# Written order of the tail columns and the first output products, one transfer for the last block

## The chip, the cores and the metric

The kernel runs on one core of one Trainium2 chip. The metric is the device time of one execution in microseconds (us). Before the change three timed runs gave 408.18, 406.88 and 407.25 us, a median of 407.25 us. Beside them one more execution was profiled; every row below is of that one.

## The reference

Three layers follow each other on 4 batches of 576 tokens, all in 32-bit floats: an attention through 32 memory slots per head, an expert layer in which each token has one of 8 experts, and a gated feed-forward layer. The change is in the third layer, and in the second a load of the first is cut in two. Cut to what matters:

```python
# attention, per batch and head (q, k, v: 576 x 64, phi: 576 x 32)
a = softmax(phi over the tokens);  k_m, v_m = a.T @ k, a.T @ v
x = softmax(q @ k_m.T / 8) @ v_m                  # 8 heads side by side: 576 x 512
# experts: e is the token's own best, or that of the token before it
x[s] = p[e] * (relu(x[s] @ w1[e]) @ w2[e])        # 512 -> 1024 -> 512
# gated layer
h = relu(x @ w_in)                                # 512 -> 1024 columns
conv = sum over k of conv_w[k] * h[s + k - 1]     # 3 taps along the tokens, zero at both ends
out = (h * sigmoid(conv)) @ w_out                 # 1024 -> 512
```

## The kernel before

**How the work is tiled.** Every product with 32-bit accuracy is three matmuls: an operand is split into a high part (rounded, by ScalarE) and a low part (the rest, by VectorE, in a few places by GpSimd), and high times high, high times low and low times high are added up (`split`, L153, and `matmul3`, L157). For most tiles the low part is thus ready some time after the high one. The expert layer leaves its result in DRAM (`ydram`), 512 rows by 576 tokens per batch.

**The gated stage** (`gated`, L1048) handles a batch in two steps. `columns` (L1072) makes the 1024 columns of `h` in eight groups of 128, f = 0 to 7: twelve matmuls into one bank `pi0_f` of PSUM for batch 0, an eviction with relu (L1085), three taps (L1066, L1068, L1069), a sigmoid (L1098), a product (`gate`, L1099), and a split of the result into the tile `g0_f` (L154 the high part, L155 the low). Then `product` (L1141) multiplies the eight tiles `g` with `w_out`: per chunk c of 128 tokens eight groups of three matmuls into a bank `po0_c`. The bank is evicted (L1173) and stored (L1175).

**The tail.** A batch has 576 tokens, and a main block takes 512 of them. The last 64 of all four batches (with two neighbours each, 264 columns) are done together, after the main columns of batch 0: eight groups of twelve matmuls into banks `pit_0` to `pit_7`, with their own evictions `htt` (L1085), taps and splits into `tail` and `edge`. The banks of `pi0` and `pit` share four buffers, so `pit_5` must wait until `pit_1` has been evicted. The token at the edge of a main block is copied into `g` from `edge` by GpSimd (`close_main`, L1121); only the last chunk of 128 tokens, c = 3, reads it.

**What sets the order.** Each engine works through its own queue in order, and a waiting instruction holds up all behind it. Up to the gated stage the matmuls' order is written out in a table. In the gated stage a scheduler places the instructions by its own estimate of when their operands are ready, unless `tc.keep_in_program_order` holds them to the order of the code (`pin`). Before the change the main columns of batch 0 and the whole products of batch 3 are held so; the tail's columns and the first products of batch 0 are not, and the scheduler mixes them. Products of c = 0 to 2 with f = 0 to 5 may run before the tail is done.

**Loads of the attention.** `load_kv` (L348) brings keys and values, 1 MB for each of 8 units; units 0 to 3 come in two transfers, the others in one.

**The end.** The last block (batch 3, c = 3) goes into a bank of its own, `last`. Behind a branch for a case that doesn't arise here (`more`, L1188) ScalarE evicts it in two halves of 256 columns (L1198), and SyncE stores each half (L1199).

Of the kernel before, what the change touches and what calls it, by code (L numbers as in the profile page):

```python
# [117 lines left out]
def fused_kernel(tc, q, first, first_q, kv, kv_tail, phi, w1, w2, w_in, conv_w, w_out, out):  # L118
# [3 lines left out]
    with (  # L122
# [225 lines left out]
        def load_kv(u):  # L348

            t = kvs[u] = ap.tile([128, 4, 4, 128], F32, tag="kv", bufs=KB, name=f"kv{u}")  # L350
            with behind(needed_behind(u // 2)):
                if u < 4:
                    for i in range(2):
                        nc.sync.dma_start(t[:, 2 * i:2 * i + 2].rearrange("p c h n -> p (c h n)"), kv[u, i])
                else:
                    nc.sync.dma_start(t.rearrange("p (i c) h n -> p i (c h n)", i=2), kv[u].rearrange("i p n -> p i n"))
                if u % 2 == 0:

                    ends[u // 2] = ap.tile([128, 4, 128], F32, tag="kt", bufs=2, name=f"kt{u // 2}")
                    nc.sync.dma_start(ends[u // 2].rearrange("p h n -> p (h n)"), kv_tail[u // 2])  # L360
# [549 lines left out]
        def load_y(b, e):  # L910

            y = state.tile([128, 4, S], F32, tag="ay", name=f"y{b}")
            nc.sync.dma_start(y[:, :, :MT], ydram[b].rearrange("d p s -> p d s")[:, :, :MT])
            return y[:, :, :MT], load_p(b, e, b, MT)[:, :MT] if e is not None else None
# [14 lines left out]
        def split_tails(yp, nm):  # L929
            y, p = yp  # L930
            t = state.tile([128, 2, 4, B * TW], F32R, tag="ay", name=f"ts{nm}")
            parts = [t[:, i] for i in range(2)]
            if p is not None:
                nc.vector.tensor_tensor(y, y, p.rearrange("p (o s) -> p o s", o=1).to_broadcast([128, 4, B * TW]), ALU.mult)
            split(*parts, y)
            return parts
# [111 lines left out]
        def gated(gp, nm, scaled=False):  # L1048
            def first(b):
                return None if scaled else expert(b)  # L1050
# [56 lines left out]
            for b in range(B):  # L1107
# [13 lines left out]
                def close_main(f):  # L1121
                    nc.gpsimd.tensor_copy(gs[f][:, :, MT - 1:], edge[:, f, :, b:b + 1].bitcast(F32))
# [2 lines left out]
                    while len(wo) < 4 and f >= WO[len(wo)]:  # L1125
                        wo.append(w2_piece(f"wo{len(wo)}", slow(f"wo.{len(wo)}")))

                columns(f"{nm}{b}", ys, store_main, tc.keep_in_program_order if b == 0 else lambda ins: ins, between)
                if b == 0:
                    tails = split_tails(tails, nm)  # L1130
                    yn = load_y(1, first(1))
                    columns(f"{nm}t", tails, store_tail)
                    for f in range(8):
                        close_main(f)
                if b + 1 < B:
                    ys = y_parts(b + 1)
                    split_y(b + 1, yn, *ys)

                pin = tc.keep_in_program_order if b == B - 1 else lambda ins: ins

                def product(ps, c, fr):  # L1141
                    for f in fr:
# [5 lines left out]
                                                                    start=f == 0 and i == 0, stop=f == 7 and i == 2)).ins]  # L1148

                chunks = [0, 1, 2] + [4] * (b % 2) + [3]  # L1150
                pss = {c: bank(f"po{b}_{c}") for c in chunks[:3]}
                for c in chunks[:3]:
                    product(pss[c], c, range(0, 6))
                for c in chunks:
                    if c in pss:
                        product(pss[c], c, range(6, 8))
# [31 lines left out]
        with tc.If(any_more > 0, preferred_fallthrough_block=True, label="more"):  # L1188
# [3 lines left out]
                    other_experts(b)  # L1192
            with tc.tile_pool(name="again", bufs=8, reuse_waits="tile") as gp:
                gated(gp, "x", True)
        for cq in range(2):
            cols = slice(256 * cq, 256 * cq + 256)
            ot = late[1].tile([128, 256], F32, tag="last", bufs=2, name=f"ot_{cq}")
            nc.scalar.activation(ot, last_block[0][:, cols], AF.Copy)  # L1198
            nc.sync.dma_start(out[B - 1, 384:512, cols], ot)  # L1199
        last_cm[0].__exit__(None, None, None)  # L1200
        late[0].__exit__(None, None, None)

# [50 lines left out]
```

## Time and profile before

| what | us |
|---|---|
| profiled execution, whole | 406.64 |
| its span, first to last instruction | 404.8 |
| median of the three timed runs | 407.25 |
| TensorE busy (matmuls) | 397.6 |
| VectorE busy | 282.9 |
| ScalarE busy | 228.1 |
| GpSimd busy | 65.4 |

The profiled execution is 1.84 us longer than its span. It is 0.61 us below the median of the timed runs. TensorE is PE in the rows, its weight loads PEld, VectorE DVE, ScalarE ACT, GpSimd POOL, and SyncE's queue, which issues most transfers, SPq. A row of a timeline gives the start in us from the start of the span, the duration in us, the engine, the line, the operation with the tile it writes and those it reads, and in brackets how long the engine was idle before it and what ended that. PE works through the columns and products of batch 0 and the tail from 204 to 259 us.

### The profile page before, as it was taken

How to read it: one execution, taken by the hardware profiler on the slowest of the kernel's cores; microseconds unless marked ns; L12 is line 12 of the kernel's file. 1: busy time of each engine (PE TensorE's matmuls, PEld its weight loads, DVE VectorE, ACT ScalarE, POOL GpSimd, SP SyncE). 2: the span in 40 equal slices, each digit the busy share in tenths (PEclk: the TensorE clock that was granted, in tenths of full speed). 3: DMA queues.
4: the chain of work that ended last, by engine and by line, in shares of the span. 5: the costliest groups of instructions: out<-in, count | busy, mean ns of one | idle time of the engine just before them, and what ended most of it. 6: DMA issues, size and time to landing. Idle time of an engine off the chain costs nothing. (4 is left out here: it accounts for less than half of the span.)

```text
span 404.8 us, 7759 instructions
## 1 busy us (share of the span) xinstructions
PE 397.6 (98%) x2969; PEld 344.2 (85%) x2970; DVE 282.9 (70%) x545; ACT 228.1 (56%) x457; POOL 65.4 (16%) x128
## 2 busy tenths in 40 slices
PE   7999999999999999999999999999999999999996
PEld 3469989899989998999988988888888888888884
DVE  3689898897868996786868999479600895069500
ACT  4466567565576366465757748468422882268311
POOL 1000201412023211311100313304100041002200
PEclk9999999999999999999999999999999999999999
DMA  7999988999196959945313033200011000200022
GB/s 265 350 397 406 361 276 307 407 414 413 46 324 211 373 147 400 389 162 171 105 61 115 26 105 104 104 2 1 2 78 52 2 0 0 104 2 0 3 80 57
DMA packets 26525, 69.03 MB, mean 171 GB/s; under 512 B 5904, under 2 KB 6672, under 8 KB 26480
## 3 DMA queue, kind: packets, MB, share of 16 engines
q1 hardware_dynamic: 22896, 56.92, 39.4%
q0 software_dynamic: 3584, 11.54, 7.2%
q8 instruction: 25, 0.41, 0.4%
q14 instruction: 20, 0.16, 0.1%
HBM read 52.12 MB, written 16.33 MB: 169 GB/s over the span
## 5 line engine op out<-in xcount | busy, mean ns | idle before, releaser
L167 PE MATMUL py<-h,wb 128*128 128x288 f32 x768 | 104.7, 296 | 0.0
L167 PEld LDWEIGHTS py<-h,wb 128*128 128x128 f32 x768 | 102.4, 188 | 0.7 <-issue 0.5
L1147 PE MATMUL po<-wo,g 128*128 128x512 f32 x360 | 83.0, 390 | 0.0
L167 PE MATMUL pi<-yh,wi 128*128 128x512 f32 x256 | 79.5, 389 | 0.0
L1147 PEld LDWEIGHTS po<-wo,g 128*128 128x128 f32 x360 | 67.4, 188 | 14.0
L167 PEld LDWEIGHTS pi<-yh,wi 128*128 128x128 f32 x256 | 48.1, 188 | 10.0
L1068 DVE SCALAR_TENSOR_TENSOR ct<-ht,convw,ct 128x510 f32<-128x510 f32 x32 | 23.9, 747 | 45.7 <-ACT ct L1066 45.7
L167 PE MATMUL ph<-att,vh 128*128 128x288 f32 x256 | 52.7, 300 | 0.0
L167 PE MATMUL pi<-yl,wi 128*128 128x512 f32 x128 | 49.8, 389 | 0.0
L167 PEld LDWEIGHTS ph<-att,vh 128*128 128x128 f32 x256 | 40.7, 188 | 2.8 <-ACT h L809 0.8
L894 POOL DMA_DIRECT2D ydram<-ys x32 | 18.0, 561 | 144.4 <-ACT ys L893 131.1
L167 PE MATMUL ph<-att,vl 128*128 128x288 f32 x128 | 37.5, 294 | 0.0
L809 ACT ACTIVATE h<-ph 128x288 fp32r<-128x288 f32 x64 | 25.6, 410 | 18.3 <-PE ph L167 17.9
L810 DVE SCALAR_TENSOR_TENSOR h<-ph,h 128x288 fp32r<-128x288 f32 x64 | 27.9, 449 | 9.4 <-ACT h L809 9.1
L1173 ACT ACTIVATE ot<-po 128x512 f32<-128x512 f32 x17 | 9.9, 597 | 41.5 <-PE po L1147 41.5
L155 POOL TENSOR_TENSOR g<-ct,g 128x511 fp32r<-128x511 f32 x12 | 16.3, 1362 | 105.0 <-ACT g L154 105.0
L893 ACT ACTIVATE ys<-py 128x288 f32<-128x288 f32 x32 | 13.1, 409 | 32.8 <-issue 16.6
L1069 DVE SCALAR_TENSOR_TENSOR ct<-ht,convw,ct 128x511 f32<-128x511 f32 x32 | 30.4, 951 | 0.5
L1085 ACT ACTIVATE ht<-pi 128x512 f32<-128x512 f32 x32 | 19.0, 594 | 20.5 <-PE pi L167 20.5
L167 PEld LDWEIGHTS pi<-yl,wi 128*128 128x128 f32 x128 | 24.0, 188 | 4.9
L154 ACT ACTIVATE g<-ct 128x511 fp32r<-128x511 f32 x32 | 19.7, 626 | 13.7 <-DVE ct L1099 13.3
L1099 DVE TENSOR_TENSOR ct<-ht,ct 128x511 f32<-128x511 f32 x32 | 23.5, 734 | 5.3 <-ACT ct L1098 5.0
(250 smaller groups left out, 556.3 us busy)
## 6 DMA issues: line engine op xcount, KB each, us to landing
q<-in_q SPq DMA_DIRECT2D x8, 576.0 KB, 10.0
ydram<-ys POOLq DMA_DIRECT2D x32, 144.0 KB, 5.0
kv<-in_kv SPq DMA_DIRECT2D x8, 512.0 KB, 6.9
kv<-in_kv SPq DMA_DIRECT2D x4, 1024.0 KB, 10.4
y<-ydram SPq DMA_DIRECT2D x4, 1024.0 KB, 5.8
out<-ot SPq DMA_DIRECT2D x15, 256.0 KB, 2.0
ph<-in_phi SPq DMA_DIRECT2D x8, 288.0 KB, 6.8
adram<-at POOLq DMA_DIRECT2D x8, 288.0 KB, 6.4
```

Source lines behind the costliest of these rows:

```text
L154: pin(nc.scalar.activation(hi, src, AF.Copy))
L155: pin((eng or nc.vector).tensor_tensor(lo, src, hi.bitcast(F32), ALU.subtract))
L167: pin(nc.tensor.matmul(ps, st, mv[:, cols], start=i == 0, stop=i == len(terms) - 1))
L809: nc.scalar.activation(t[:, 0, :], ps, AF.Relu)
L810: low = nc.vector.scalar_tensor_tensor(t[:, 1, :], ps, 0.0, t[:, 0, :].bitcast(F32), ALU.max, ALU.subtract)
L893: nc.scalar.activation(yt, ps, AF.Copy)
L894: stored.append(nc.gpsimd.dma_start(ydram[b, d, :, half(hf)], yt).ins)
L1068: nc.vector.scalar_tensor_tensor(ct[..., a:], ht[..., :n - a], w(0), ct[..., a:], ALU.mult, ALU.add)
L1069: nc.vector.scalar_tensor_tensor(ct[..., :more], ht[..., first + 1:first + 1 + more], w(2), ct[..., :more], ALU.mult, ALU.add)
L1085: nc.scalar.activation(ht, ps, AF.Relu)
L1099: slow(f"gm.{f}").tensor_tensor(ct, own, ct, ALU.mult)
L1147: last_product[:] = [pin(nc.tensor.matmul(ps, st[sp], w[:, mp, f % 2, :], start=f == 0 and i == 0, stop=f == 7 and i == 2)).ins]
```

## The change

Three edits. First, the products of batch 0 are held to the written order like those of batch 3, and so are the tail's columns. The 18 groups that may run early (c = 0 with f = 0 to 5, then c = 1, then c = 2) are handed out in portions: eight of them behind the tail's column group 2, five behind group 5, and the other five after the tail. Second, the last block is evicted in one pass of 512 columns and stored in one transfer of 256 KB. Third, unit 4 of keys and values is loaded in two transfers instead of one.

```diff
             with behind(needed_behind(u // 2)):
-                if u < 4:
+                if u < 5:
...
-                columns(f"{nm}{b}", ys, store_main, tc.keep_in_program_order if b == 0 else lambda ins: ins, between)
-                if b == 0:
-                    tails = split_tails(tails, nm)
-                    yn = load_y(1, first(1))
-                    columns(f"{nm}t", tails, store_tail)
-                    for f in range(8):
-                        close_main(f)
-                if b + 1 < B:
-                    ys = y_parts(b + 1)
-                    split_y(b + 1, yn, *ys)
-
-                pin = tc.keep_in_program_order if b == B - 1 else lambda ins: ins
+                pin = tc.keep_in_program_order if b in (0, B - 1) else lambda ins: ins
...
                 chunks = [0, 1, 2] + [4] * (b % 2) + [3]
-                pss = {c: bank(f"po{b}_{c}") for c in chunks[:3]}
-                for c in chunks[:3]:
-                    product(pss[c], c, range(0, 6))
+                pss = {}
+
+                def products_ahead(n):
+
+                    for _ in range(n):
+                        c, f = divmod(ahead_of.pop(0), 6)
+                        if c not in pss:
+                            pss[c] = bank(f"po{b}_{c}")
+                        product(pss[c], c, [f])
+
+                ahead_of = list(range(18))
+
+                columns(f"{nm}{b}", ys, store_main, tc.keep_in_program_order if b == 0 else lambda ins: ins, between)
+                if b == 0:
+                    tails = split_tails(tails, nm)
+                    yn = load_y(1, first(1))
+                    columns(f"{nm}t", tails, store_tail, pin, lambda f: products_ahead({2: 8, 5: 5}.get(f, 0)))
+                    for f in range(8):
+                        close_main(f)
+                if b + 1 < B:
+                    ys = y_parts(b + 1)
+                    split_y(b + 1, yn, *ys)
+
+                products_ahead(len(ahead_of))
...
-        for cq in range(2):
-            cols = slice(256 * cq, 256 * cq + 256)
-            ot = late[1].tile([128, 256], F32, tag="last", bufs=2, name=f"ot_{cq}")
-            nc.scalar.activation(ot, last_block[0][:, cols], AF.Copy)
-            nc.sync.dma_start(out[B - 1, 384:512, cols], ot)
+        ot = late[1].tile([128, DM], F32, tag="last", bufs=1, name="ot")
+        nc.scalar.activation(ot, last_block[0], AF.Copy)
+        nc.sync.dma_start(out[B - 1, 384:512, :], ot)
```

Two places show what moves. The first is TensorE's queue, from the end of the tail's column group 2 (`pit_2`) to the start of group 3 (`pit_3`). `po0_0` and `po0_1` are the banks of batch 0's chunks 0 and 1, `g0_f` the gated tiles, `wo` the pieces of `w_out`; a trailing number only counts buffers. Before:

```order
L167 MATMUL pit_2_3300<-ts_3248,wi3_2928 128x264 x3
L1147 MATMUL po0_0_3478<-wo0_3111,g0_0_3076 128x512 x3
L1147 MATMUL po0_0_3478<-wo0_3111,g0_1_3100 128x512 x3
L1147 MATMUL po0_0_3478<-wo1_3162,g0_2_3135 128x512 x3
L1147 MATMUL po0_0_3478<-wo1_3162,g0_3_3159 128x512 x3
L1147 MATMUL po0_0_3478<-wo2_3189,g0_4_3186 128x512 x2
L1147 MATMUL po0_1_3479<-wo0_3111,g0_0_3076 128x512 x3
L1147 MATMUL po0_1_3479<-wo0_3111,g0_1_3100 128x512 x3
L1147 MATMUL po0_1_3479<-wo1_3162,g0_2_3135 128x512
L1147 MATMUL po0_0_3478<-wo2_3189,g0_4_3186 128x512
L167 MATMUL pit_3_3325<-ts_3248,wi0_2769 128x264 x3
```

The same stretch of TensorE's queue now:

```order
L167 MATMUL pit_2_3301<-ts_3249,wi3_2929 128x264 x3
L1136 MATMUL po0_0_3326<-wo0_3112,g0_0_3077 128x512 x3
L1136 MATMUL po0_0_3326<-wo0_3112,g0_1_3101 128x512 x3
L1136 MATMUL po0_0_3326<-wo1_3163,g0_2_3136 128x512 x3
L1136 MATMUL po0_0_3326<-wo1_3163,g0_3_3160 128x512 x3
L1136 MATMUL po0_0_3326<-wo2_3190,g0_4_3187 128x512 x3
L1136 MATMUL po0_0_3326<-wo2_3190,g0_5_3214 128x512 x3
L1136 MATMUL po0_1_3345<-wo0_3112,g0_0_3077 128x512 x3
L1136 MATMUL po0_1_3345<-wo0_3112,g0_1_3101 128x512 x3
L167 MATMUL pit_3_3352<-ts_3249,wi0_2770 128x264 x3
```

The block has 24 matmuls instead of 22, and the three that read `g0_5`, which stood behind `pit_5`, are now the 16th to 18th of it. The next block, between `pit_5` and `pit_6`, goes from 18 matmuls to 15, and the one behind `pit_7` up to the next batch from 56 to 57, of which the first matmul of batch 1's columns (`pi1_0`) has moved ahead of the last two groups of chunk 3.

The second place is VectorE's queue at the end of the tail, where `y3` is batch 3's input, scaled in four pieces (L943), and `edge` and `tail` are low parts of the tail's results. Before:

```order
L1099 TENSOR_TENSOR ctt_7_3441<-htt_7_3440,ctt_7_3441 128x260
L943 TENSOR_TENSOR y3_3949<-y3_3949,p3_3951 128x512 x2
L155 TENSOR_TENSOR edge_3025<-ctt_6_3416,edge_3025 128x4
L943 TENSOR_TENSOR y3_3949<-y3_3949,p3_3951 128x512 x2
L155 TENSOR_TENSOR tail_3024<-ctt_7_3441,tail_3024 128x256
L155 TENSOR_TENSOR edge_3025<-ctt_7_3441,edge_3025 128x4
```

The same stretch of VectorE's queue now:

```order
L1099 TENSOR_TENSOR ctt_7_3484<-htt_7_3483,ctt_7_3484 128x260
L943 TENSOR_TENSOR y3_3950<-y3_3950,p3_3952 128x512 x4
L155 TENSOR_TENSOR edge_3026<-ctt_6_3459,edge_3026 128x4
L155 TENSOR_TENSOR tail_3025<-ctt_7_3484,tail_3025 128x256
L155 TENSOR_TENSOR edge_3026<-ctt_7_3484,edge_3026 128x4
```

The low part of the edge of column group 6 moves behind all four pieces of `y3`. Apart from this and from the last eviction, ScalarE's, VectorE's and GpSimd's queues have the same order as before in all that is executed.

## Rows read from the trace of the kernel before

**Rows 1.** The page, busy time: engine, us (share of the span), instructions.
```profile
PE 397.6 (98%) x2969; PEld 344.2 (85%) x2970; DVE 282.9 (70%) x545; ACT 228.1 (56%) x457; POOL 65.4 (16%) x128
```

**Rows 2.** Waits of PE from 20 to 405 us: total, times, longest.
```profile
PE pv L474 <- DMA wa_1r<-in_w: 0.3, 1, 0.3
```

**Rows 3.** Timeline of PE, batch 0's products and the tail's columns.
```profile
229.86 5.19 PE L1147 MATMUL po<-wo,g 128*128 128x512 f32 x22
234.89 4.85 PE L167 MATMUL pit<-ts,wi 128*128 128x264 f32 x36
239.57 4.26 PE L1147 MATMUL po<-wo,g 128*128 128x512 f32 x18
243.67 3.08 PE L167 MATMUL pit<-ts,wi 128*128 128x264 f32 x24
246.59 12.92 PE L1147 MATMUL po<-wo,g 128*128 128x512 f32 x56
```

**Rows 4.** Timeline of PEld in the same stretch.
```profile
229.74 4.88 PEld L1147 LDWEIGHTS po<-wo,g 128*128 128x128 f32 x22
...
237.99 1.52 PEld L167 LDWEIGHTS pit<-ts,wi 128*128 128x128 f32 x12 [0.22 <-ACT htt L1085]
```

**Rows 5.** Timeline of ACT: the high part of g0_5, evictions htt_1 and htt_3.
```profile
233.85 0.63 ACT L154 ACTIVATE g<-ct 128x511 fp32r<-128x511 f32 x1 [1.60 <-DVE ct L1099]
...
237.57 0.37 ACT L1085 ACTIVATE htt<-pit 128x264 f32<-128x264 f32 x1
...
244.61 0.37 ACT L1085 ACTIVATE htt<-pit 128x264 f32<-128x264 f32 x1
```

**Rows 6.** Timeline of DVE: batch 1's input, and the low part of g0_5.
```profile
220.39 2.50 DVE L943 TENSOR_TENSOR y<-y,p 128x512 f32<-128x512 f32 x4 [1.20 <-DMA y<-ydram]
...
235.06 0.67 DVE L155 TENSOR_TENSOR g<-ct,g 128x511 fp32r<-128x511 f32 x1
```

**Rows 7.** DVE's L1069 from 211 to 237 us and tile yl: ns min/median/max, starts.
```profile
L1069 DVE SCALAR_TENSOR_TENSOR ct<-ht,convw,ct x8: 735/746/1789, 210.5 to 235.7; 128x511 f32<-128x511 f32 x8
L155 DVE TENSOR_TENSOR yl<-y,yh x4: 677/678/1782, 229.0 to 231.9; 128x512 fp32r<-128x512 f32 x4
```

**Rows 8.** Tile y, 205 to 262 us: issues of its loads, time to landing.
```profile
L913 SPq DMA_DIRECT2D y<-ydram x3: 359/359/360, 213.9 to 246.8; - x3
DMA to landing us min/median/max: 5.2/5.2/6.4
```

**Rows 9.** Timeline of DVE and POOL at the end of the tail.
```profile
254.23 1.78 DVE L943 TENSOR_TENSOR y<-y,p 128x512 f32<-128x512 f32 x2
257.76 0.79 POOL L1122 CAST g<-edge 128x2 fp32r<-128x2 f32 x6 [1.03 <-DVE edge L155]
```

**Rows 10.** Stretches: busy us of each engine, then granted clock, DMA share, GB/s.
```profile
5.00:7.00 2.00, 1.52 (x14) 1.09 (x18) 1.17 (x7) 1.90 (x6) 0.00 (x0) 1.00 0.87 237
401.20:404.80 3.60, 0.00 (x0) 0.00 (x0) 0.00 (x0) 0.66 (x2) 0.00 (x0) 0.85 0.22 73
```

**Rows 11.** The end: last evictions, and stores of the halves with time to landing.
```profile
401.25 0.66 ACT L1198 ACTIVATE ot<-last 128x256 f32<-128x256 f32 x2 [4.93 <-PEq L1188]
L1199 SPq DMA_DIRECT2D out<-ot x2: 337/354/371, 401.7 to 402.1; - x2
DMA to landing us min/median/max: 1.7/1.7/1.8
```

**Rows 12.** Evictions of 512 columns, and landing of the 256 KB stores (L1175).
```profile
L1173 ACT ACTIVATE ot<-po x17: 581/598/602, 254.8 to 395.7; 128x512 f32<-128x512 f32 x17
DMA to landing us min/median/max: 2.0/2.0/2.4
```

**Rows 13.** Unit 4 of keys and values: its load's issue, its first use.
```profile
34.20 0.39 SPq L356 DMA_DIRECT2D kv<-in_kv  x1
57.46 1.08 PE L430 MATMUL pk<-kv,a 128*32 128x128 f32 x32
```

## The prediction

> **What bounds the kernel now.** I read the page's busy times first: TensorE is busy for 397.6 of 404.8 us, VectorE for 282.9 [rows 1]. Then the waits of TensorE, to see whether that share hides any idle time: from 20 us to the end there is one, of 0.3 us [rows 2]. So TensorE goes from the first products of the expert layer to the last matmul practically without a gap, and every microsecond by which its queue is held up in between comes out at the end. Only its own timeline and the arrival of its operands matter, and I read the stretch in which the change moves matmuls. There the reader is to see three kinds of rows: the blocks on TensorE and their pace [rows 3], the one wait of its weight loads [rows 4], and when ScalarE and VectorE finish what those matmuls read [rows 5, 6].
>
> The pace: 22 products from 229.86 to 234.89 us are 0.2286 us each, and 24 tail matmuls from 243.67 to 246.59 us are 0.1217 us each [rows 3]. The 36 tail matmuls from 234.89 to 239.57 us took 4.68 us, while 36 times 0.1217 is 4.38. The missing 0.30 us belong to a wait of 0.22 us for the eviction of pit_1 [rows 4], whose ScalarE row ends at 237.57 + 0.37 = 237.94 us [rows 5]; the next weight load starts 0.05 us later. So such a wait costs its length and some 0.08 us for getting going again.
>
> **The first block: a new wait.** The block now has 24 matmuls, and the 16th to 18th read g0_5; before, they stood behind pit_5, at 239.57 us. Without a wait the weights of the 16th would be loaded at 229.74 + 15 x 0.2286 = 233.17 us. But the high part of g0_5 is written by ScalarE from 233.85 to 234.48 us, and there ScalarE had itself waited for VectorE [rows 5]. The queue is in order, so TensorE stands until 234.48 + 0.05 = 234.53 us: 1.36 us. The 17th needs only the high part. The 18th would then load at 234.53 + 2 x 0.2286 = 234.99 us, but VectorE writes the low part from 235.06 to 235.73 us [rows 6], so it loads at 235.78 us: another 0.79 us. Two waits, 2.15 us, and with 0.08 us each for getting going again 2.31 us. Behind the waiting matmul stand the six products of c = 1, then pit_3 to pit_5, and all the rest.
>
> Could g0_5 come earlier? The order on ScalarE, VectorE and GpSimd is unchanged up to there, and what they wait for doesn't hang on the moved matmuls: VectorE's chain to g0_5 begins at 220.39 us, when batch 1's input landed, after an idle time of 1.20 us [rows 6]. So I take 2.31 us. From below: that load took up to 6.4 us to land where others of the line took 5.2 [rows 8], and with 1.2 us less the two waits shrink to 0.95 us, 1.1 with the restarts. From above: each wait with a whole row of its producer more behind it (0.63 and 0.67 us), if these slip, 3.6 us.
>
> **The first block: a wait that goes.** TensorE reaches pit_3 at 229.86 + 24 x 0.2286 + 2.31 = 237.66 us and pit_5 after 24 tail matmuls, at 240.58 us. The eviction of pit_1 ended at 237.94 us, so the old wait is gone: 0.30 us back. What is late next? pit_6 and pit_7 need the banks of pit_2 and pit_3. The block between them now has 15 products, so it runs from 237.66 + 36 x 0.1217 = 242.04 to 245.47 us, and pit_7 starts at 246.93 us; pit_3 was evicted from 244.61 us for 0.37 us [rows 5], and pit_2 before it. Neither waits, since ScalarE's evictions lagged far behind TensorE already and don't wait for the later matmuls. If they did slip, the nearest price is the old wait of 0.22 us. The tail ends at 248.39 us instead of 246.59: 1.80 us later.
>
> **Batch 3's input and the edges: nothing.** Its load frees its slot only when pit_7 is done. It was issued at 246.8 us [rows 8], now at 248.6, and lands 5.2 to 6.4 us later [rows 8], at 253.8 to 255.0 us. VectorE came to it at 254.23 us [rows 9], so it may wait up to 0.8 us, and behind it stand the edges of column groups 6 and 7, and behind those GpSimd's copies, of which that of group 7 was the first of those at 257.76 us [rows 9]. They slip to about 258.8 us at the most. The products that read them, the last two groups of c = 3, start at 248.39 + (33 + 18 + 1) x 0.2286 = 260.28 us. That is 1.5 us of cover; only a load 1.5 us slower than the slowest of its line would be felt, at its excess.
>
> **The end: nothing.** Before, the two halves were evicted from 401.25 to 401.91 us, and their stores were issued at 401.7 and 402.1 us and landed 1.7 to 1.8 us later, the last at 403.8 us [rows 11]. One pass of 512 columns takes 0.598 us [rows 12]; it ends at 401.85 us, its store is issued some 0.02 us later, and one of 256 KB landed in 2.0 us [rows 12]: 403.87 us, so +0.07 us. Bounds: 1.7 us to land gives -0.23, the slowest of 2.4 gives +0.47.
>
> **Unit 4's load: nothing.** One issue more of 0.39 us at 34.20 us; TensorE first reads it at 57.46 us without waiting [rows 13]. Half a load sooner gains nothing, and those 23 us hide whatever the queue behind it slips. If that cover were gone, its price would be the one issue, 0.39 us; from below, 0.
>
> **Sum.** 2.31 - 0.30 + 0.07 = +2.08 us. On the profiled execution that is 406.64 + 2.08 = 408.7 us; the median of the runs stands 0.61 us above that execution, so I forecast 407.25 + 2.08 = 409.3 us.
>
> **The clock.** In the waits TensorE stands 2.15 us out of some 2.6. Between 5 and 7 us it was busy for 1.52 us of 2 and the granted clock stayed at 1.00, the level of 2.4 GHz; in the last 3.6 us, with nothing on it, the mean was 0.85, so part of that at the other level, 1.2 GHz [rows 10]. The new gap lies between. The Trainium skill (TensorE: Matmul & The Clock Gate, The HAM clock gate) says that the low clock is the default and that activity alone releases it, so idle gaps inside a kernel can bring half speed back. By that rule the gap is dangerous, by the first row it is harmless; the rows decide neither, which gives the last rival below.
>
> **Rivals.** (1) The load of batch 1's input lands sooner than in the profiled execution, and the wait is half as long: 1.1 - 0.30 + 0.07 = +0.9, 408.1 us. For it: 5.2 us was the median. Against: it is issued behind the same work as before. (2) Not slower: g0_5 is ready in time. That needs its low part 2.15 us sooner, and VectorE has the room: 1.20 us idle, one L1069 that took 1.79 instead of 0.75 and one low part of batch 1's input that took 1.78 instead of 0.68 [rows 7], 3.3 us in all. From 2.15 us on the new wait is nothing, the old one of 0.30 is gone as well, and with the end's -0.23 it gives 406.7 us. Against: at least two of the three would have to change, and no edit touches them. (3) The change does nothing: the blocks were 22, 18 and 56 and are 24, 15 and 57, and if the three moved groups had slack that the rows don't show, 407.2 us. Against: the end times of the two writes are plain rows. (4) The clock falls in the gap. Priced as if the rest of the first block and half of the tail matmuls behind it (7 x 0.2286 + 18 x 0.1217 = 3.8 us) took twice as long, +5.9 us, 413.1 us; with only the seven products, 410.9.
>
> **How the numbers follow.** Chances: the forecast 0.68, (1) 0.13, (2) 0.06, (3) 0.06, (4) 0.07. A measurement of this kernel tells about 0.3% from no change, 1.2 us: slower is above 408.5 us, faster below 406.0. The forecast's own range is 408.4 to 410.1 us and lies nearly all in slower, as does (4); (1) to (3) lie within 0.3%, and only (2) with a low run reaches faster. Slower 0.70, same 0.26, faster 0.04. The range is 407.3 to 410.3 us: it takes in (1) and the forecast, and leaves out (2), most of (3) and (4).
>
> **What would show it.** Right: between 233 and 236 us TensorE's weight loads wait twice in the products, for ScalarE's and for VectorE's write of g0_5, about 1.4 and 0.8 us; no wait for an eviction of the tail; the tail ends 1.8 us later and the rest is moved by that alone; at the end one eviction and one store that landed at the old distance from the last matmul, within 0.3 us. Wrong: no wait at g0_5, or a wait there that VectorE's rows place well before 235 us; a granted clock below 1.00 behind the gap; a wait for GpSimd's copies in chunk 3. If the tail ends at its old time, the forecast has failed, whatever the total is.

## The result: 0.6% slower, as forecast, and the profile after

| | before | after |
|---|---|---|
| median of 20 runs each | 406.94 us (406.13 to 408.18) | 408.97 us (407.42 to 411.5) |
| ratio, after to before | | 1.0061, 95% interval 1.0049 to 1.0073 |
| profiled execution | 406.64 us, span 404.8 | 408.6 us, span 406.9 |

The medians differ by 2.03 us and the two profiled spans by 2.0 (2.1 as rounded in the table); forecast was +2.08. The change is slower by more than 0.3%.

First the waits of TensorE after 20 us (total, times, longest), which answer to [rows 2]. Beside a short wait of the opening (0.2 us) there are now two, both in the output products (`po`), for the two writes of a `g` tile:

```profile
PE po L1136 <- ACT g L154: 1.0, 1, 1.0
PE po L1136 <- DVE g L155: 0.5, 1, 0.5
```

TensorE's timeline (start, us, instructions, idle time before and who ended it) answers to [rows 3]:

```profile
230.04 3.60 PE L1136 MATMUL po<-wo,g 128*128 128x512 f32 x15
234.65 0.73 PE L1136 MATMUL po<-wo,g 128*128 128x512 f32 x2 [1.01 <-ACT g L154]
235.91 1.88 PE L1136 MATMUL po<-wo,g 128*128 128x512 f32 x7 [0.53 <-DVE g L155]
237.63 4.57 PE L167 MATMUL pit<-ts,wi 128*128 128x264 f32 x36
242.04 3.56 PE L1136 MATMUL po<-wo,g 128*128 128x512 f32 x15
245.43 3.10 PE L167 MATMUL pit<-ts,wi 128*128 128x264 f32 x24
248.37 11.76 PE L1136 MATMUL po<-wo,g 128*128 128x512 f32 x51
```

The block of 24 is broken after the 15th and the 17th matmul, which is where g0_5's high part and then its low part are read. It lasts from 230.04 to 237.63 us, 7.59 us, where 24 at the pace of before (0.2286 us) would take 5.49: held up by 2.10 us. The 36 tail matmuls behind it take 4.41 us where they took 4.68: the wait for pit_1's eviction is gone. The tail ends at 248.37 us; before it was 246.59.

The weight loads, which go ahead of the matmuls, show the longer side of the same waits. They answer to [rows 4]:

```profile
234.65 0.30 PEld L1136 LDWEIGHTS po<-wo,g 128*128 128x128 f32 x2 [1.44 <-ACT g L154]
235.91 1.46 PEld L1136 LDWEIGHTS po<-wo,g 128*128 128x128 f32 x7 [0.96 <-DVE g L155]
```

Who came late stands in the timelines of ScalarE and VectorE, against [rows 5] and [rows 6]. ScalarE's high part again waits 1.59 us for VectorE, and VectorE again idles 1.09 us until batch 1's input lands; all rows are within 0.13 us of where they were:

```profile
233.97 0.63 ACT L154 ACTIVATE g<-ct 128x511 fp32r<-128x511 f32 x1 [1.59 <-DVE ct L1099]
```
```profile
220.51 2.50 DVE L943 TENSOR_TENSOR y<-y,p 128x512 f32<-128x512 f32 x4 [1.09 <-DMA y<-ydram]
...
235.18 0.68 DVE L155 TENSOR_TENSOR g<-ct,g 128x511 fp32r<-128x511 f32 x1
```

And the end, the tile of the last block (durations in ns, starts in us), against [rows 11]:

```profile
L1206 ACT ACTIVATE ot<-last x1: 597/597/597, 403.3 to 403.3; 128x512 f32<-128x512 f32 x1
L1207 SPq DMA_DIRECT2D out<-ot x1: 338/338/338, 403.9 to 403.9; - x1
...
DMA to landing us min/median/max: 2.0/2.0/2.0
```

The store lands at 405.9 us, 2.0 us later than before. So nearly the whole difference of the spans is there when the tail ends (1.78 us); 0.23 us more is one product that is now done behind the tail instead of ahead of it, and under 0.1 us is the end: from the end of the last matmul to the landing of the last store it is 2.73 us before and 2.76 after.

In the profiled execution the granted clock stayed at 1.00 through the gap. It didn't in all of them: of the 20 runs of after, six show a mean clock of .994 to .996 over the whole execution, and these took 409.85 to 411.5 us. The other 14 have a median of 408.73 us, 1.79 us above before.

### The profile page after: what moved, and what is told of

Its sections match the earlier page's. It is cut to its first block, busy times and chain, and to the rows that moved or that the text cites. A ratio compares the mean times of both kernels' runs of the same rounds, so it can differ in the third digit from the quotient of the medians.

```text
span 406.9 us, 7757 instructions
## 1 busy us (share of the span) xinstructions
PE 398.6 (98%) x2969; PEld 344.4 (85%) x2970; DVE 282.9 (70%) x545; ACT 228.2 (56%) x456; POOL 65.4 (16%) x128
## 5 line engine op out<-in xcount | busy, mean ns | idle before, releaser
L893 ACT ACTIVATE ys<-py 128x288 f32<-128x288 f32 x32 | 13.1, 410 | 33.2 <-issue 16.7
L1069 DVE SCALAR_TENSOR_TENSOR ct<-ht,convw,ct 128x511 f32<-128x511 f32 x32 | 30.4, 950 | 0.5
```

The source lines that it names most:

```text
L893: nc.scalar.activation(yt, ps, AF.Copy)
L1069: nc.vector.scalar_tensor_tensor(ct[..., :more], ht[..., first + 1:first + 1 + more], w(2), ct[..., :more], ALU.mult, ALU.add)
```

## The experiments

All were timed in rounds with the kernel before on the same chip. The ratio is to that kernel, with its 95% interval; "the two waits" are those of TensorE's weight loads for g0_5, and "clock" is a run's mean granted clock. A diff is against the changed kernel unless another is named, and `...` marks what is left out. In every profile but one_group_earlier's the first block of products begins 26.20 us behind the first matmul of the gated stage, but that matmul comes at 203.3 to 204.8 us, in profiles without matmuls added at the start; so two profiles are best compared over the stretch from the first block to the end of the tail.

### The parts of the change, alone and in pairs

**order_alone**: only the new written order; the other two edits are taken back.

```diff
-                if u < 5:
+                if u < 4:
...
-        ot = late[1].tile([128, DM], F32, tag="last", bufs=1, name="ot")
+        for cq in range(2):
+            cols = slice(256 * cq, 256 * cq + 256)
+            ot = late[1].tile([128, 256], F32, tag="last", bufs=2, name=f"ot_{cq}")
...
```

> The kernel before with the written order alone: two eviction halves and two stores at the end, unit 4 loaded in one transfer. My theory (TensorE waits for the two writes of g0_5, 2.3 us, and loses the old wait of 0.3 us): +2.0 us against before, ratio 1.005, with two waits of 1.4 and 1.0 us of the weight loads near 234 us. Rival (the other two edits carry a part, by the end or by the transfers' order): clearly less than the whole change's +2.1 us of span, and nothing like +2.0.

Measured 407.47 us (12 runs), ratio 1.0022 (1.0007 to 1.0037). The sign is right, the size is not. In its profile batch 1's input was there when VectorE came to it: the row has no idle time, where after has 1.09 us, and starts 1.5 us sooner. So the two waits, shown under it, are half as long (1.1 us in sum against 2.4):

```profile
218.97 2.49 DVE L943 TENSOR_TENSOR y<-y,p 128x512 f32<-128x512 f32 x4
```
```profile
PEld po L1136 <- DVE g L155: 1.0, 1, 1.0
PEld po L1136 <- ACT g L154: 0.2, 1, 0.2
```

That is rival (1) of the prediction, in one execution.

**end_and_load**: the other two edits, in the scheduler's order of before. The diff is against the kernel before.

```diff
-                if u < 4:
+                if u < 5:
...
-        for cq in range(2):
-            cols = slice(256 * cq, 256 * cq + 256)
...
+        ot = late[1].tile([128, DM], F32, tag="last", bufs=1, name="ot")
+        nc.scalar.activation(ot, last_block[0], AF.Copy)
+        nc.sync.dma_start(out[B - 1, 384:512, :], ot)
```

> The kernel before with the other two edits alone: one eviction and one store of 256 KB at the end, unit 4 in two transfers; the scheduler's order of the products stays. My theory: +0.07 us, between -0.25 and +0.5, ratio 0.9995 to 1.001. Rival (these edits carry a part of the slowdown): +0.5 us or more.

Measured 406.83 us (12 runs), ratio 1.0008 (0.9998 to 1.0019). These two edits cost nothing that can be told from no change. The slowdown is the written order's. One more thing stands in this profile: the scheduler's order of before has no wait for the eviction of pit_1 here. The input landed after 6.1 us instead of before's 6.4, that eviction ended at 237.66 us instead of 237.94, and the 36 tail matmuls took 4.44 us instead of 4.68. So the old wait, too, hung on when batch 1's input landed.

**order_and_end** and **order_and_load**: the written order with one of the other two edits each.

```diff
order_and_end:
-                if u < 5:
+                if u < 4:
order_and_load:
-        ot = late[1].tile([128, DM], F32, tag="last", bufs=1, name="ot")
+        for cq in range(2):
+            cols = slice(256 * cq, 256 * cq + 256)
+            ot = late[1].tile([128, 256], F32, tag="last", bufs=2, name=f"ot_{cq}")
...
```

> The changed kernel with unit 4's load in one piece again (new written order and one store at the end). Theory A (the wait for g0_5 is all that costs; when batch 1's input lands varies from execution to execution and hangs on no load of unit 4): about the written order alone plus nothing for the end, +0.8 to +2.0 us over the kernel before, the two waits of TensorE's weight loads together 1.2 us where the input is early and 2.4 us where it is late. Theory B (the split of unit 4's load makes batch 1's input land late, so that the whole costs more than its parts): here the input lands early, VectorE multiplies it at about 219 us without waiting for the DMA, the waits are 1.2 us, +0.8 us.

> The changed kernel with the last block's two evictions and two stores as before (new written order and unit 4's load in two pieces). Theory A: the same as order_and_end within 0.5 us, +0.8 to +2.0 us over the kernel before. Theory B: batch 1's input lands late, VectorE waits about 1 us for it before 220.5 us, the two waits are 2.4 us, and the time is that of the whole change, +2.0 us and more, 1.2 us over order_and_end.

order_and_end took 408.16 us (406.99 to 410.11, 12 runs), ratio 1.0030 (1.0011 to 1.0050); order_and_load 410.04 us (408.75 to 411.29, 6 runs), ratio 1.0077 (1.0051 to 1.0102). In both profiles the input landed late (6.4 and 6.5 us after its issue), with the two waits at 2.4 and 2.6 us. So theory B as I wrote it falls: without the split of unit 4's load the input can land late too. But the times don't agree with theory A either, which wanted both equal within 0.5 us. With the split load the written order costs 0.6 to 0.8% (also in after), without it 0.2 to 0.3%. The pair here, timed together, is the only direct comparison, and its two intervals barely part (up to 1.0050, from 1.0051); block_into_load below costs 0.48% without the split. The experiments on the landing, below, say what this may be; it isn't settled.

### The wait itself

**gap_filled**: the changed kernel, with 5 and 3 matmuls of no use where TensorE would stand.

```diff
+                            if nm == "" and (b, c, f) == (0, 0, 5) and i != 1:
+                                fill(5 if i == 0 else 3)
```

> The changed kernel with 8 matmuls of 128x512 more, 5 ahead of the first matmul on g0_5 and 3 ahead of its third; they write into the bank of c = 1 before its own products start and overwrite it, so nothing of them is used. They stand where TensorE would wait. My theory: the wait is the operand's, so filling it changes nothing: span 406.9 us within 0.2, with TensorE busy through the gap. Second question, the clock: six of the 20 runs of the changed kernel list a mean granted clock of 0.994 to 0.996 and take 409.9 to 411.5 us. If the gap lets the clock fall, the filled one lists 1.00 in all runs, none is above 410 us, and its median is about 0.5 us below the changed kernel's 408.97. If the clock falls for another reason, some of its runs list 0.994 as well.

Measured 408.92 us (6 runs), ratio 1.0049 (1.0031 to 1.0067). TensorE's timeline shows the same block with the idle time turned into work (L1147 are the added matmuls):

```profile
229.48 3.60 PE L1138 MATMUL po<-wo,g 128*128 128x512 f32 x15
232.92 1.30 PE L1147 MATMUL po<-wo,g 128*128 128x512 f32 x5
234.05 0.67 PE L1138 MATMUL po<-wo,g 128*128 128x512 f32 x2
234.56 0.86 PE L1147 MATMUL po<-wo,g 128*128 128x512 f32 x3
235.26 1.87 PE L1138 MATMUL po<-wo,g 128*128 128x512 f32 x7
236.97 4.56 PE L167 MATMUL pit<-ts,wi 128*128 128x264 f32 x36
```

The block lasts 236.97 - 229.48 = 7.49 us against 7.59 with the wait, so this prices the wait for g0_5 without TensorE's idle time: 0.49% of 406.7 us is 2.0 us. From the block to the end of the tail it is 18.22 us against after's 18.33; the input landed 0.15 us sooner here (6.13 against 6.28 us). The span, 406.1 us, missed the forecast of 406.9 within 0.2: the stage began at 203.28 us, 0.55 us sooner than in after. All six runs show a clock of .998 or more and none is above 409.34 us, while after goes to 411.5. That fits a gap that lets the clock fall. The times alone don't show it: the median isn't 0.5 us below the changed kernel's, as I had forecast, but 408.92 against 408.97, and the intervals of the two ratios overlap.

**one_group_earlier**: the block of eight one tail group sooner, so that TensorE comes to g0_5 1.46 us earlier.

```diff
-products_ahead({2: 8, 5: 5}.get(f, 0))
+products_ahead({1: 8, 5: 5}.get(f, 0))
```

> The changed kernel with the first block of eight products one tail group earlier: twelve tail matmuls fewer stand ahead of it. Theory A: the writes of g0_5 stay where they are and TensorE reaches them 12 x 0.1217 = 1.46 us sooner, so the waits grow by 1.46 us to 3.6 to 3.9 us, and the twelve matmuls are only moved behind the block: +1.5 us over the changed kernel, about 410.5 us. Rival (TensorE reads the block's other operands or waits for something else there, and g0_5 is not what holds it): no change of more than 0.5 us. On the clock: if it is the length of the gap that lets the granted clock fall, more runs than the six of twenty of the changed kernel show a mean of .996 or less; if it is chance that hits any kernel, about none, as with the kernel before.

Measured 412.13 us (411.83 to 412.53, 5 runs), ratio 1.0124 (1.0099 to 1.0148): 5.0 us, not the 3.5 that theory A gave. All five runs show a clock of .992 to .996. The profile has both parts. The waits are 3.9 us, 1.5 longer, as theory A said; 0.2 of that is for g0_4, whose low part GpSimd makes:

```profile
PEld po L1136 <- ACT g L154: 2.9, 1, 2.9
PEld po L1136 <- DVE g L155: 0.8, 1, 0.8
PEld po L1136 <- POOL g L155: 0.2, 1, 0.2
```

and in a table of stretches (length, busy time of PE, PEld, DVE, ACT and POOL, granted clock, DMA share, GB/s) TensorE is busy for 0.90 us of the three from 232 us, and the granted clock falls to 0.57 in the four behind them, near the level of 1.2 GHz, and is back at 1.00 behind them. As an estimate, the whole change's 2.5 us (0.61%), 1.5 of wait and 1.0 for a clock that now falls in every run instead of a third of them (1.56 us each, after_again below) make the 5.0:

```profile
232.00:235.00 3.00, 0.90 (x4) 0.35 (x2) 3.00 (x5) 1.32 (x3) 0.35 (x1) 1.00 0.15 13
235.00:239.00 4.00, 3.41 (x7) 2.25 (x8) 3.63 (x7) 3.25 (x7) 0.31 (x1) 0.57 0.70 252
239.00:245.00 6.00, 6.00 (x49) 5.89 (x48) 6.00 (x11) 2.30 (x6) 0.99 (x1) 1.00 0.01 3
```

**g5_later**: the changed kernel with g0_5's product of c = 0 moved to the second block; the sizes of the blocks stay.

```diff
-                ahead_of = list(range(18))
+                ahead_of = [0, 1, 2, 3, 4, 6, 7, 8, 5, 9, 10, 11, 12, 13, 14, 15, 16, 17]
```

> The changed kernel with one entry of the written order moved: the products of c = 0 with f = 5 go from the first block to the start of the second, and c = 1 with f = 2 comes forward in their place; the sizes of the blocks stay 24, 15 and 57. My theory: no wait in the first block and none for the eviction of pit_1 or one shorter than 0.2 us: -2.3 us of span against the changed kernel, 404.6 us, and -0.2 us against before, ratio 0.9995, within 0.3%. Rival (the written order itself, its block sizes or its pinning costs the time): stays at +2 us against before. Clock: if the gap makes the clock fall in some executions, the runs here list a mean granted clock of 1.00 like those of before, not 0.994.

Measured 407.47 us (12 runs), ratio 1.0016 (1.0005 to 1.0028), no clock below .998. The wait for g0_5 is gone, and 0.45% with it. The rest, some 0.6 us, I didn't expect. In part it is a wait of the weight loads in pit_7 for its bank, which stands in no other profile of the written order and cost 0.39 us of the 24 tail matmuls (3.33 us, where after took 2.94):

```profile
PEld pit L167 <- ACT htt L1085: 0.3, 1, 0.3
```

From the block to the end of the tail the profile has 16.61 us with 39 products, where before had 16.73 with 40: 0.11 us more, once the product (0.23) is taken off. And its gated stage began at 204.39 us, 0.73 us later than before (203.66) and 0.56 later than in after (203.83), upstream of anything that the edit touches. Whether the other runs began late as well isn't known, so the rest of this cost stays open.

**input_behind_g5**: the changed kernel, with VectorE's scaling of batch 1's input put behind the low part of g0_5. TensorE's order is untouched.

```diff
-                    with tc.issue_after(hidden_low[-1]) if b == 0 else contextlib.nullcontext():
+                    with tc.issue_after(hidden_low[-1] if b == 0 else main_low[5]) if b < 2 else contextlib.nullcontext():
```

> The changed kernel with one thing more: the scaling of batch 1's input on VectorE is put behind the low part of g0_5, so that VectorE does the chain of g0_5 without waiting for that input; TensorE's order is the changed kernel's. Theory A: VectorE's part of g0_5 comes some 6 us sooner (the input's rows between 220.5 and 230 us go behind it), both waits for g0_5 go, the old wait of 0.3 us stays gone, and the time is -2.4 us against the changed kernel, -0.3 us against the kernel before, about 406.6 us; the input's scaled rows come later, but TensorE reads them only after batch 0's output products. Rival (the order on VectorE alone brings the wait elsewhere, since the evictions of the tail on VectorE or ScalarE slip behind): waits of the same length reappear in the tail, and no more than 0.8 us are won.

Measured 406.92 us (12 runs), ratio 0.9993 (0.9979 to 1.0006). The same order on TensorE costs nothing once VectorE does g0_5 first:

```profile
231.03 5.64 PE L1138 MATMUL po<-wo,g 128*128 128x512 f32 x24
236.50 4.57 PE L167 MATMUL pit<-ts,wi 128*128 128x264 f32 x36
240.91 3.56 PE L1138 MATMUL po<-wo,g 128*128 128x512 f32 x15
244.31 3.10 PE L167 MATMUL pit<-ts,wi 128*128 128x264 f32 x24
247.25 11.76 PE L1138 MATMUL po<-wo,g 128*128 128x512 f32 x51
```

From 231.03 to 247.25 us there are 16.22 us; before, with one product more, 16.73 [rows 3]. Less that product (0.23) the stretch is 0.28 us shorter: the old wait of 0.30. That confirms the prediction's second term by itself. It also shows that the new wait needs two things: TensorE's new order, and VectorE's work on batch 1's input ahead of g0_5. Without the second the first costs nothing that can be told from no change.

### When batch 1's input lands

**blocks_before_load** (24 matmuls of 32 columns, of no use, at the very start of the changed kernel; the diff is of this one) and **block_into_load** (8 of them in order_and_end).

```diff
+            if n == 8 and i == 0:
+                for _ in range(24):
+                    nc.tensor.matmul(idle[i][:, :32], ident_r, ident_r[:, :32], start=True, stop=True)
```

> The changed kernel with 24 more matmuls of 32 columns, of no use, in the idle time at the very start. What it asks: why batch 1's input lands after 5.1 us in one profile and after 6.1 to 6.5 us in the nine others. In each of them one 16 KB block of TensorE's program is fetched through the DMA engines (queue q8, 1.05 us on one of them) around that load: 2.5 to 4.3 us after its issue in the nine, 4.54 us after it in the one, and in the nine the last packets trickle at 23 GB/s behind the rest. Theory F (the fetch holds up one DMA engine, and that engine's share of the load lands last): the 48 instructions more bring the fetch some 5.5 us sooner, to 210.5 to 212.5 us, ahead of the issue at about 214 us; the input lands after 5.1 to 5.3 us, VectorE doesn't wait for it, the waits for g0_5 are 1.2 us together, and the time is 1.2 us or more below the changed kernel's of this call. Rival (the landing is chance, or hangs on the load's own addresses): the fetch moves, the input still lands after 6.1 us or more, and the time stays.

> Written order and one store at the end, unit 4's load in one piece, with 8 such matmuls at the start. Without them the fetch came 4.29 us after the issue in the profile, near the end of the load, and the kernel took +1.25 us over the kernel before. Theory F: 16 instructions more bring the fetch 1.8 us sooner, to about 2.5 us after the issue, where it always hits the load: the input lands after 6.1 us or more in every execution, the waits are 2.4 us, and the time is that of the whole change in this call, +1.7 to +2.6 us over the kernel before. Rival (unit 4's load in two pieces is what makes the whole dearer than its parts, and the fetch has nothing to do with it): +1.2 us as without the matmuls.

blocks_before_load took 412.79 us (6 runs), ratio 1.0132 (1.0105 to 1.0158): the 24 matmuls were not free, they took 5.9 us of the opening and the gated stage began 6.6 us later than in after, so its time says nothing here. Its profile answers the question: the fetch came 4.1 us ahead of the input's issue, the input landed after 5.1 us, VectorE didn't wait, and the two waits were 1.3 us. block_into_load took 408.96 us (407.22 to 409.95, 6 runs), ratio 1.0048 (1.0031 to 1.0066). There I had the shift wrong: the fetch came 4.6 us sooner, not 1.8, and fell 0.3 us ahead of the issue; the input landed after 5.1 us, and that execution was the shortest of its six. Its other five took 408.27 to 409.95 us, all at a clock of .998 or more, and where the fetch fell in them isn't known. As a test of the rival it is void.

Over the 14 profiles, with the time of the fetch of TensorE's program block (queue q8) read from narrow stretches of the DMA's view:

| fetch against the input's issue, us | landing, us | profiles |
|---|---|---|
| 2.5, 2.6, 2.8, 2.8, 3.1, 3.3, 3.5, 3.9, 4.3, 4.3 after | 6.1 to 6.5 | 10 |
| 4.5, 4.5 after | 5.1 | 2 (blocks_24_18_54, order_alone) |
| 0.3, 4.1 ahead | 5.1 | 2 (block_into_load, blocks_before_load) |

In the DMA's view of before the block, one packet, stands in the half microsecond from 217.5 us: 13.1% of 16 engines over 0.5 us is 1.05 us of one engine. The 16 engines moved the load's packets at 97.7% in that time, and single packets still dribble behind 218.5 us, a slice here and there at 33 GB/s (the second line, 218.5 to 221 us in 40 slices):

```profile
q1 hardware_dynamic: 93, 0.19, 97.7%
q8 instruction: 1, 0.02, 13.1%
```
```profile
GB/s 0 0 0 0 0 33 0 0 33 0 0 0 33 0 0 33 0 33 33 0 33 0 0 0 0 0 0 0 0 0 0 0 0 0 0 0 0 0 0 0
```

In order_alone, where the block came only at 218.3 us, the stretch from 218.7 us has nothing left:

```profile
DMA packets 0, 0.00 MB, mean 0 GB/s; under 512 B 0, under 2 KB 0, under 8 KB 0
```

order_and_load is the plainest case. The load was issued at 213.63 us, and the block, fetched from 217.98 us, took 1.08 us. From 218.25 to 219.00 us no packet starts, and then one does, the load's last, at 219.05 us, as the block ends (the views of 218.25 to 219.00 us and of 219.00 to 219.20):

```profile
DMA packets 0, 0.00 MB, mean 0 GB/s; under 512 B 0, under 2 KB 0, under 8 KB 0
DMA packets 1, 0.00 MB, mean 0 GB/s; under 512 B 1, under 2 KB 1, under 8 KB 1
```

So the landing follows the fetch in all 14, and here one packet of the load stands behind the block while all others are done. The Trainium skill (Runtime: NRT & Kernel Launch, Instruction fetch mechanics) says that programs are fetched in 16 KiB blocks over an engine's own DMA queue and that crossing into a new one is mostly hidden. For TensorE that holds here, whose list has no wait at that time in any of the 14 profiles; a load that shares the DMA engine lands 1.0 to 1.4 us later.

It may also be why the split of unit 4's load matters: without matmuls added at the start, the fetch came 14.1 to 14.7 us behind the first matmul of the gated stage in the four profiles without the split, close to the border of the table and early in two of the four, and 12.9 to 13.8 us behind it in seven of the eight with it (14.6 in the last), with the input late in all eight. Why a split load should move the fetch no run shows, and how often the input is early in executions without a profile of their own isn't known. This stays open.

### The change once more, and a version without the wait

**after_again** is the changed kernel itself, so it has no diff.

> The changed kernel once more, on the chip and in the call of the next three, for comparison. Both theories: +0.4 to +0.7% over the kernel before; batch 1's input lands 6.1 to 6.5 us after its issue, and the two waits for g0_5 are 2.4 us together.

Measured 409.84 us (6 runs), ratio 1.0063 (1.0043 to 1.0083). Its profile caught an execution of 411.43 us with a mean clock of .994, where that of after had .998:

```profile
234.00:237.00 3.00, 1.29 (x5) 0.43 (x3) 3.00 (x6) 1.43 (x3) 0.00 (x0) 1.00 0.65 162
237.00:241.00 4.00, 3.93 (x13) 3.25 (x14) 3.56 (x6) 2.54 (x5) 1.28 (x1) 0.57 0.36 141
241.00:245.00 4.00, 4.00 (x34) 3.95 (x34) 4.00 (x9) 1.47 (x4) 0.00 (x0) 1.00 0.02 4
```
```profile
230.96 3.60 PE L1136 MATMUL po<-wo,g 128*128 128x512 f32 x15
235.80 0.74 PE L1136 MATMUL po<-wo,g 128*128 128x512 f32 x2 [1.25 <-ACT g L154]
237.07 3.20 PE L1136 MATMUL po<-wo,g 128*128 128x512 f32 x7 [0.53 <-DVE g L155]
240.06 4.86 PE L167 MATMUL pit<-ts,wi 128*128 128x264 f32 x36
244.76 3.60 PE L1136 MATMUL po<-wo,g 128*128 128x512 f32 x15
```

The gap is 0.24 us longer than in after (the two waits are 2.64 us). Behind it the clock is at half for some three of the four microseconds, seven products take 2.99 us where after's took 1.72, and the 36 tail matmuls 4.70 where they took 4.41: 1.56 us in all.

**blocks_24_18_54**: the kernel before with the written order, but g0_5's first product in the second block and one product more there. Not shown in the diff: unit 4's load and the end are as before the change.

```diff
-                ahead_of = list(range(18))
+                ahead_of = [0, 1, 2, 3, 4, 6, 7, 8, 5, 9, 10, 11, 12, 13, 14, 15, 16, 17]
...
-products_ahead({2: 8, 5: 5}.get(f, 0))
+products_ahead({2: 8, 5: 6}.get(f, 0))
```

> A version that might beat both: the written order, with c = 0's product of g0_5 and those behind it placed so that the first block is 24 matmuls (g0_5 not among them), the second 18, the third 54; unit 4's load and the two halves at the end as before the change. From the rows of before: no wait for g0_5, since its product comes only in the second block; the first block's two more products of c = 1 cover the eviction of pit_1, so the old wait of 0.3 us goes: -0.3 us against the kernel before, and no granted clock below .998. If waits reappear in the last two tail groups, as the 0.3 us of the kernel with g0_5 later did, 0.

Measured 406.61 us (12 runs), ratio 0.9989 (0.9978 to 1.0000), no clock below .998, and no wait in the stage:

```profile
230.41 5.64 PE L1136 MATMUL po<-wo,g 128*128 128x512 f32 x24
235.88 4.57 PE L167 MATMUL pit<-ts,wi 128*128 128x264 f32 x36
240.29 4.24 PE L1136 MATMUL po<-wo,g 128*128 128x512 f32 x18
244.37 3.10 PE L167 MATMUL pit<-ts,wi 128*128 128x264 f32 x24
247.31 2.92 PE L1136 MATMUL po<-wo,g 128*128 128x512 f32 x12
```

From 230.41 to 247.31 us it takes 16.90 us with 42 products, where before took 16.73 with 40: 0.29 us less once the two products (0.46) are taken off. It beats the changed kernel. Against the kernel before the 12 runs give -0.11%, with an interval that reaches to no change; the 0.3 us that there were to win are 0.07%.

## Why the prediction was right, point by point

**The new wait (+2.31).** Right in place, order and cause: two waits of the weight loads at 233 to 236 us, forecast at 1.36 and 0.79 us, measured at 1.44 and 0.96. But what TensorE was held up is 2.10 us, less than these 2.40. I had added 0.08 us per wait for getting going again, after the old wait of pit_1, where the loss was larger than the wait of the weight load; here it was smaller, and the matmuls' own idle time (1.54 us) smaller still. The term of 2.31 us is some 0.2 us too large.

**The wait that goes (-0.30).** Right: 4.68 became 4.41 us, and input_behind_g5 shows it alone. But it is a price of executions in which the input lands late; end_and_load, where it landed 0.3 us sooner, has no such wait in the old order.

**The tail ends 1.80 us later.** It ended 1.78 us later, but not by the terms alone: the first block began 0.18 us later, before anything that the change moves, and the stretch itself grew by 1.60. The error of the term above and this shift cancel. A forecast for one execution can't be better than such shifts. That the medians differ by 2.03 us where +2.08 was forecast is luck in part: without the six runs with a lower clock, which the sum has at nothing, it would be 1.79.

**The edges, unit 4's load, the end.** No wait for GpSimd's copies or for batch 3's input shows in TensorE's list; the end took +0.03 us, where +0.07 was forecast. For the two smaller edits end_and_load bounds the cost at 0.19%. One step wasn't thought of: that the split load, which costs nothing alone, may make the written order dearer (0.6 to 0.8% with it, 0.2 to 0.3% without).

**The rivals.** (1), the shorter wait, is real: it stood in order_alone, and in the two kernels with matmuls added at the start (block_into_load, blocks_before_load); in both profiles of the changed kernel itself the input was late. (2), g0_5 in time, was never seen until input_behind_g5 made it so. (3) fell with the rows. (4), the clock, I gave 0.07; the clock was .996 or less in 9 of 26 runs of the changed kernel (six of 20, three of six). So one of the prediction's own signs of being wrong, a granted clock below 1.00 behind the gap, came in a third of the runs. Its time was met at the lower of its two prices: 410.9 us "with only the seven products", measured a median of 410.96 us in the nine against 408.74 in the other 17. That is 2.2 us apart, where after_again's profile accounts for 1.56; the rest isn't explained. As a share of runs rather than an alternative to the forecast it adds 9/26 of 1.56, 0.5 us, to the mean, which is about what stands between gap_filled's 0.49% and the 0.61 and 0.63% of after, though those intervals overlap.

**What was shown and what not.** That the wait for g0_5 makes the slowdown is shown from three sides: without its idle time it costs the same (gap_filled), with VectorE's chain turned round it is gone with its cost (input_behind_g5), and with TensorE there 1.5 us sooner it is longer by about that and dearer still by the clock (one_group_earlier). That the fetch sets the landing rests on 14 profiles that agree, not on a time. That the clock falls because of the gap rests on the count of runs with and without it. What unit 4's split does to the landing is open, and so is part of g5_later's 0.16%.

## What to carry to other kernels

When an order is written out by hand for an engine that is always busy, put each step against the end of the row that writes its operand, not against the order of the producers: here one operand 1.4 us late, and its second part another 1.0, held up all behind them for 2.1 us. Look behind the producer for what it waited for itself; here it was work on the next batch's input, early in VectorE's order and not needed yet, and moving that behind g0_5 took the whole cost away without touching TensorE's order. And price a gap in TensorE with the clock behind it, as a share of executions.

## What the runs showed of the hardware

A gap of 2.4 to 2.6 us in the weight loads, with TensorE idle for 1.5 to 1.8 us in the two profiles, came with a fall of the granted clock to the level of 1.2 GHz in a third of the changed kernel's runs (9 of 26) and not in the others, at the same place in the program; one of 3.9 us did so in 5 of 5, and in the five kernels without such a gap (end_and_load, g5_later, gap_filled, input_behind_g5, blocks_24_18_54) the clock fell in none of 54 runs. The four other kernels whose profiles show the gap at full or half length had a mean clock of .996 or less in 5 of 36 runs (order_alone 1 of 12, order_and_end 2 of 12, order_and_load 2 of 6, block_into_load none of 6), and blocks_before_load, with its longer opening, in 3 of 6. The kernel before shows .996 once in the 69 runs beside the experiments, in the slowest (408.52 us) of the 23 timed with order_and_end. The gap's length alone doesn't tell which execution it hits: the clock stayed at 1.00 behind waits of 2.58 us in order_and_load's profile and fell behind 2.64 us in after_again's. At half speed it stayed for some 3 us and cost 1.6 us. The Trainium skill (TensorE: Matmul & The Clock Gate, The HAM clock gate) has idle gaps bring the low clock back; the runs agree, but with the same program only some of the time.

One block of TensorE's program, fetched in the middle of a load of 1 MB, goes with a landing between 6.1 and 6.5 us after the issue instead of 5.1, and by the chain behind it with twice the wait of TensorE 15 us later (2.4 us against 1.1).
